# The fourth batch of a fused FFT filter and expert layer does two steps of its last stage per slot, and counts and places in one slot

## The chip, the cores and the metric

The kernel runs on one core of one Trainium2 chip. The metric is the device time of one execution in microseconds (us), the median of several runs. The profile is of one further execution. PE is TensorE, DVE is VectorE, ACT is ScalarE, POOL is GpSimd and SP is SyncE; SP does nothing here but start DMA transfers.

## The reference

Each of 8 batches holds 2496 tokens of 256 channels. A circular filter runs over the tokens of a batch, and every filtered token then goes to one of 8 experts.

```python
X = np.fft.rfft(x, axis=1)                       # x: 8 x 2496 x 256
y = np.fft.irfft(X * (filt_r + 1j*filt_i), n=2496, axis=1)
x = y.reshape(8*2496, 256)                       # 19968 tokens
logits = x @ w_gate + modality_bias[modality_id] # 8 experts
e_idx = np.argmax(logits, axis=1)
probs = softmax(logits); gate_w = probs[arange, e_idx]
for e in range(8):
    mask = e_idx == e
    h = np.maximum(x[mask] @ w1[e], 0.0)         # 256 -> 1024
    out[mask] = gate_w[mask, None] * (h @ w2[e]) # 1024 -> 256
```

## The kernel before, in words

The batches are numbered 0 to 7, so the fourth batch is batch 3. A batch of 2496 = 48 x 52 tokens passes through three stages of small transforms.

- **Stage 1** (13 steps): PE multiplies the input rows (L245), ACT moves the result out of PSUM (L249) and stores it to DRAM (`b1_d`, L252).
- **Stage 2** (12 pairs of frequencies, 13 steps): SP loads `t2` back from `b1_d` (L534), PE transforms forward (`forward`, L551), ACT evicts (L578), DVE multiplies by the filter (L585, L586), PE transforms back (`inverse`, L563 and L564), ACT evicts `z` (L614) and stores it to `b2_d` (L616).
- **Stage 3** (10 working steps and 2 that drain): SP loads `t4` from `b2_d` (L540, four pieces of 8, 8, 8 and 2 columns, each good for three steps, the last for one). Each step does four matmuls (L688, L691) into a PSUM tile, scales it into the token rows `yo` (DVE L726 in even steps, ACT L724 in odd ones), transposes the tokens of the step before (PE L711, DVE copy `yT` L720), and adds the gate's logits of the step before that (PE L716, DVE L729).

Then the routing of the batch: **count** (`counting`, L737 to L757, a chain of small DVE operations over all 20 columns of logits: maximum, one-hot, running count `c`), **place** (`placing`, L763 to L785: a pair of matmuls L765 and L766 that sums `c` over the partitions into the PSUM tile `psO`, then positions on DVE; the exponential on ACT, L767), and **table** (`tabling`, L832 to L868: which blocks of 256 tokens are full). After it, POOL scatters the batch's 20 tiles of tokens into the bins of the experts in DRAM (`bins_d`, L806, an indirect DMA each, of 128 rows of 520 bytes).

The **experts** take blocks of 256 tokens from the bins: SP loads `xs` (L914), PE transposes (L951), DVE copies (L952) and copies the block's first weight matrix (L933), PE multiplies (`up`, L965), ACT applies the ReLU (L970), PE multiplies again (`down`, L978), DVE scales by the gate weight into `osb` (L990), and POOL writes the rows out (L992, an indirect DMA).

Batches 0 to 2 pass through another form of the stages first. From there a loop over slots `n` interleaves what is left (at the end of the code below). In each slot one step of stage 1 of a batch, one of stage 2 of an earlier one, one of stage 3 of a still earlier one, some scatters and one or two of the experts' steps are issued. `begin[g]` is a batch's first slot, -15 for batch 3 and `(g-4)*14` for the later ones; stage 2 begins `OFF2` = 17 slots later and stage 3 `OFF3` = 34 slots later. So batch 3 has its stage 3 in slots 19 to 30, counts in slot 31, and places and tables in slot 32; its scatters are issued in slots 32 to 45. Batch 4 begins stage 3 in slot 34. The experts take two steps per slot before slot 24 and 1.25 on average from there on (`EARLY`, `STEPS`).

The slot loop gives the work in program order; a scheduler then sets the order on each engine from it, and waits on semaphores tie the engines together. DMA transfers started by ACT and SP take one of eight semaphore lanes in turn (DMAHW0 to DMAHW7); a new transfer on a lane waits until the one before it on that lane has landed. The scatters have lanes of their own (DMASW0 to DMASW7). The stages share one PSUM pool, `ps`, of three buffers: stage 1, both transforms of stage 2, the step of stage 3, its transposes with the logits, and `psO` all take their tile there, five tiles in a slot before (seven with two steps of stage 3). The tiles `t2` and `t4` share four SBUF buffers, and the routing's small tiles (`lg`, `c` and the others) have one buffer each.

Of the kernel before, what the change touches and what calls it, by code (L numbers as in the profile page):

```python
# [29 lines left out]
def kernel(  # L30
# [87 lines left out]
    TURNED = 2  # L118
# [99 lines left out]
    NPY = NY // EV  # L218
# [36 lines left out]
    def input_piece(g, k):  # L255

        stage1(g, k)
        if (k + 1) * EV in [t1 for t0, t1 in TCH]:
            load_x()
# [53 lines left out]
    def to_columns(g, q, on):  # L313

        t0 = q * TQ
        m = min(TQ, NTT - t0)
        if t0 % TCM == 0 and m < TQ and g == TURNED:
            st[g]["t4", t0 // TCM] = sp.tile([P, EV, DC, P], BF16, tag="yT", bufs=2, name="t4").rearrange(
                "p t a q -> p t (a q)")[:KA]
        elif t0 % TCM == 0:  # L320
            st[g]["t4", t0 // TCM] = bp.tile([KA, TCM, D], BF16, tag="t24", name="t4")
        pool, tag = (op, "tr") if g < TURNED else (pp, "ps")
        tt = pool.tile([P, EV * D], F32, tag=tag, name="tt").bitcast(BF16)
        tv = tt.rearrange("p (i a q) -> p i a q", i=TQ, a=DC)
        for i in range(m):
            for dc in range(DC):
                mm = nc.tensor.transpose(tv[:KA, i, dc, :], st[g]["zT"][:, dc, t0 + i, :], ident)
        marks["pe"].append(mm.ins)
        dst = st[g]["t4", t0 // TCM][:, t0 % TCM:t0 % TCM + m, :]
        evict(on, dst.rearrange("p t d -> p (t d)"), tt[:KA, 0:m * D])  # L330
# [198 lines left out]
    def load_t2(g, c, part=None):  # L529
        src = b1_d[g].rearrange("t (jr s) c -> (t jr) s c", jr=4)  # L530
        if part != 1:
            st[g]["t2", c] = bp.tile([KB, SCH, D], BF16, tag="t24", name="t2")
        a, b = {None: (0, KB), 0: (0, KA), 1: (KA, KB)}[part]
        nc.sync.dma_start(st[g]["t2", c][a:b], src[a:b, c * SCH:(c + 1) * SCH, :])  # L534

    def load_t4(g, c):
        t0, t1 = TCH[c]
        src = b2_d[g].rearrange("s (jr t) c -> (s jr) t c", jr=4)
        t4 = bp.tile([KA, TCM, D], BF16, tag="t24", name="t4")
        ins = nc.sync.dma_start(t4[:, 0:t1 - t0, :], src[:, t0:t1, :])  # L540
        st[g]["t4", c] = t4
        return ins
# [78 lines left out]
    def stage2(g, k):  # L621

        if k < NK:
            ps = forward(g, k)
        if k > 0:
            pz = inverse(g, k - 1)
        if k < NK:
            filtering(g, k, taken(g, k, ps))
        if k > 0:
            returned(g, k - 1, pz)  # L630
# [156 lines left out]
    def run(steps):  # L787

        for _ in steps:
            pass  # L790

    def count(g):

        run(counting(g))

    def place(g):

        run(placing(g))
# [307 lines left out]
    def routed(g):  # L1106

        place(g)
        to_bins.append([g, 0])

    def tabled(g):

        run(tabling(g, KR[g], g == B - 1))
# [8 lines left out]
    with tc.manual_schedule(engines={ET.PE, ET.Activation, ET.DVE}):  # L1122
# [141 lines left out]
        n = -2 * LONG  # L1264
# [31 lines left out]
    OFF3 = OFF2 + NS // EV + 1 + 4  # L1296
    begin = [(g - TURNED - 2) * GAP for g in range(B)]
# [3 lines left out]
    CHORES = [3, 3, 3, 3]  # L1301
    AFT = len(COLS)
    LEAD = 2
    end = begin[B - 1] + OFF3 + NPY + 3
    assert opening and opening[0][0] == 0
    n = max(0, opening[0][1] + WAIT)
# [3 lines left out]
    n = 0  # L1310
# [3 lines left out]
    while n <= end or to_bins or opening:  # L1314
        for g in range(TURNED + 2, B):
            if 0 <= n - begin[g] < NP:
                input_piece(g, n - begin[g])
        for g in range(TURNED + 1, B):
            k = n - begin[g] - OFF2
            if k + LEAD in (-2, -1):  # L1320
                load_t2(g, 0, k + LEAD + 2)
            if (k + LEAD) % 4 == 0 and 0 < k + LEAD < NS // EV:
                load_t2(g, (k + LEAD) // 4)
            if 0 <= k <= NS // EV:
                stage2(g, k)
        if n < AFT:
            for q in COLS[n]:
                to_columns(TURNED, q, "vs"[q % 2])
                moe.step()
        for k in (2 * (n - AFT), 2 * (n - AFT) + 1):  # L1330
            if 0 <= k < NPY:
                stage3(TURNED, k, "vs"[k % 2])
        some(CHORES[n] if n < len(CHORES) else 2)
        for g in range(TURNED + 1, B):
            k = n - begin[g] - OFF3
            if (k + LEAD) % 3 == 0 and 0 <= k + LEAD < NPY:
                load_t4(g, (k + LEAD) // 3)
            if 0 <= k <= NPY + 1:
                stage3(g, k)
            if k == NPY + 2:  # L1340
                count(g)
            if k == NPY + 3:
                routed(g)
                tabled(g)
        if n <= end:
            pace(pace(2) if n % 2 or n < GAP else 1)
            owed += EARLY if n < 24 else STEPS
        else:
            pace(1 if n % 4 else 0)
            owed += FT // FQ  # L1350
        while owed >= 1:
            owed -= 1
            moe.step()
        n += 1
# [44 lines left out]
```

## Time and profile before

| | |
|---|---|
| median of 3 runs | 556.67 us (556.52 to 557.93) |
| profiled execution | 559.18 us, of which the span of the profile is 557.3 us |
| busy share of the span | PE 89%, DVE 67%, ACT 68%, POOL 70% |
| mean granted clock of TensorE | 0.957 |
| DMA | 89.86 MB, mean 161 GB/s |

The span is the time from the first to the last instruction of the profile; 1.9 us of the profiled execution lie outside it. The clock is given as a share of full speed (2.4 GHz); 0.5 is the lower of its two levels. A row of the timeline is one instruction, or several alike that follow each other on one engine (x4), with the start in us from the span's beginning and the time that it or they took; in brackets stands how long the engine sat idle before it and what ended that. PE's matmuls are pipelined: what one costs is the distance to the next start (0.11 us for 256 columns at the full clock), not its own duration. Idle time of an engine that is not the bottleneck costs nothing.

### The profile page before, as it was taken

What the parts mean: (1) busy time and instruction counts of PE and PEld (TensorE: products, weight loads), DVE (VectorE), ACT (ScalarE), POOL (GpSimd) and SP (SyncE); (2) the same over time, 40 slices, a digit from 0 to 9 for tenths busy, and PEclk for the clock granted to TensorE, in tenths of its full rate; (3) what the DMA queues carried; (4) which work ended last, traced back from release to release, by engine and by line L of the source; (5) the groups of instructions that cost most, each with busy time, mean ns of one, the idle gap of its engine ahead of it and who ended that gap; (6) DMA issues with size and microseconds to landing.
All of it is one profiled execution on the core that took longest, in us unless ns stands there. A gap on an engine that the chain in (4) does not pass through costs nothing. (4 is left out here: it accounts for less than half of the span.)

```text
span 557.3 us, 14900 instructions
## 1 busy us (share of the span) xinstructions
PE 494.1 (89%) x5012; PEld 451.8 (81%) x5012; DVE 375.1 (67%) x1130; ACT 376.3 (68%) x694; POOL 391.5 (70%) x427
## 2 busy tenths in 40 slices
PE   3788797979999699999879999898998999979994
PEld 2677686769889588999768899897988899979993
DVE  8867968746765466797767897877554465565551
ACT  4686785845888668888678777454656666656662
POOL 9743588785578732468776777777777777777775
PEclk9979888879999889999989999998999999999998
DMA  9989979778677898988886764623544445347532
GB/s 140 164 147 205 199 143 167 174 155 172 170 172 186 198 237 183 213 234 222 213 251 196 189 187 131 185 88 110 149 110 111 124 114 125 92 129 154 133 105 71
DMA packets 98265, 89.86 MB, mean 161 GB/s; under 512 B 40151, under 2 KB 81591, under 8 KB 98095
## 3 DMA queue, kind: packets, MB, share of 16 engines
q0 software_dynamic: 30112, 50.75, 40.0%
q1 hardware_dynamic: 44773, 26.60, 19.7%
q10 hardware_dynamic: 23302, 11.50, 7.7%
q8 instruction: 44, 0.72, 0.5%
q14 instruction: 34, 0.28, 0.2%
HBM read 58.82 MB, written 45.07 MB: 186 GB/s over the span
## 5 line engine op out<-in xcount | busy, mean ns | idle before, releaser
L970 ACT ACTIVATE hT<-hps 128x512 f16<-128x512 f32 x316 | 186.9, 599 | 99.8 <-PE hps L965 95.9
L992 POOL DMA_INDIRECT out_dram<-osb,metas x158 | 165.6, 1048 | 68.5 <-DVE osb L990 30.5
L806 POOL DMA_INDIRECT bins_d<-yo,pos_i x160 | 167.8, 1049 | 57.7 <-issue 26.0
L965 PE MATMUL hps<-xT,w 128*128 128x256 f16 x1264 | 199.4, 277 | 7.3 <-ACT hT L970 2.6
L965 PEld LDWEIGHTS <-w 128*128 128x128 f16 x1264 | 149.3, 145 | 14.6 <-issue 7.0
L978 PEld LDWEIGHTS <-hT 128*128 128x128 f16 x1264 | 123.7, 99 | 17.2 <-issue 5.5
L978 PE MATMUL ops<-w2sb,hT 128*128 x704 | 113.1, 275 | 0.9 <-issue 0.7
L990 DVE TENSOR_SCALAR osb<-ops,metas 128x256 f32<-128x256 f32 x158 | 69.8, 477 | 51.9 <-DMA out_dram<-osb,metas 30.5
L978 PE MATMUL ops<-w,hT 128*128 128x256 f16 x560 | 83.3, 272 | 3.2 <-DVE osb L990 3.1
L933 DVE COPY w<-w1sb 128x2048 f16 x79 | 56.0, 709 | 32.9 <-PE hps L965 30.1
L578 ACT CAST xf<-ps 104x512 f16<-104x512 f32 x96 | 57.2, 596 | 10.2 <-PE ps L551 9.2
L585 DVE TENSOR_TENSOR p<-xf,g 104x512 f16<-104x512 f16 x96 | 40.4, 421 | 25.4 <-ACT xf L578 25.1
L614 ACT CAST z<-pz 104x512 f16<-104x512 f32 x60 | 35.4, 591 | 12.8 <-PE pz L564 8.4
L586 DVE TENSOR_TENSOR xf<-xf,g 104x512 f16<-104x512 f16 x96 | 40.5, 422 | 2.5
L551 PE MATMUL ps<-t,w2m 104*104 104x256 f16 x192 | 38.8, 285 | 1.8 <-ACT t L249 0.7
L249 ACT CAST t<-ps 96x512 f16<-96x512 f32 x52 | 30.3, 582 | 13.4 <-PE ps L245 8.8
L688 PE MATMUL ps<-t,wbm 96*128 96x256 f16 x120 | 29.4, 277 | 4.8 <-DMA t<-b_d 4.4
L952 DVE COPY xT<-pT 128x512 f16<-128x512 f16 x44 | 18.6, 422 | 22.3 <-PE pT L951 22.2
L563 PE MATMUL pz<-p,a1m 104*104 104x256 f16 x120 | 30.4, 273 | 1.9 <-DVE p L585 1.7
L164 POOL DMA_DIRECT2D xt<-in_x_dram x32 | 23.5, 735 | 11.4 <-PE ps L551 8.1
L564 PE MATMUL pz<-xf,a2m 104*104 104x256 f16 x120 | 29.4, 272 | 0.9 <-DVE xf L586 0.5
L691 PE MATMUL ps<-t,wbm 96*128 96x256 f16 x108 | 27.0, 277 | 0.0
(231 smaller groups left out, 777.2 us busy)
## 6 DMA issues: line engine op xcount, KB each, us to landing
xt<-in_x_dram POOLq DMA_DIRECT2D x24, 384.0 KB
t<-b_d SPq DMA_DIRECT2D x19, 384.0 KB
b_d<-z ACTq DMA_DIRECT2D x30, 208.0 KB
xs<-bins_d SPq DMA_DIRECT2D x44, 130.0 KB
b_d<-t ACTq DMA_DIRECT2D x24, 192.0 KB
t<-b_d SPq DMA_DIRECT2D x11, 416.0 KB
w1sb<-in_moe_w_dram POOLq DMA_DIRECT2D x16, 256.0 KB
w2sb<-in_moe_w_dram POOLq DMA_DIRECT2D x8, 512.0 KB
```

Source lines behind the costliest of these rows:

```text
L551: mm = nc.tensor.matmul(ps[:KB, i, :], lhsT=w2m[:, s + i, :], rhs=st[g]["t2", s // SCH][:, s % SCH + i, :], start=True, stop=True)
L578: nc.scalar.copy(xf, ps[:KB])
L585: nc.vector.tensor_mul(p1, xf, g1[:, sl, :])
L586: nc.vector.tensor_mul(xf, xf, g2[:, sl, :])
L614: nc.scalar.copy(st[g]["z"][:, k % 2], pz[:KB])
L806: ins = nc.gpsimd.indirect_dma_start(out=bins_d[:, :], out_offset=IOA(ap=st[g]["pos"][:rows, t:t + 1], axis=0), in_=st[g]["yw"][:rows, t, ...
L933: cp = nc.vector.tensor_copy(b["w1"].rearrange("p a f -> p (a f)"), w1sb[:, ds(ej, 1)].rearrange("p o a f -> p (o a f)"))
L965: mm = nc.tensor.matmul(hps[:, k, :], lhsT=b["w1"][:, dc, ft:F:FT], rhs=b["xT"][:, dc].rearrange("p i t -> p (i t)"), start=(dc == 0), sto ...
L970: nc.scalar.activation(b["hT"][:, q * FQ:(q + 1) * FQ, :], hps, AF.Relu)
L978: nc.tensor.matmul(b["ops"][:, i, :], lhsT=b["hT"][:, ft, i * P:(i + 1) * P], rhs=b["w2"][:, ft, :] if b["still"] else w2sb[:, ds(b["e"], ...
L990: nc.vector.tensor_scalar_mul(osb[:, i, :], b["ops"][:, i, :], gate[:, i, :])
L992: ins = nc.gpsimd.indirect_dma_start(out=out[:, :], out_offset=IOA(ap=b["meta"][:, i, 0:1], axis=0), in_=osb[:, i, :], in_offset=None, bou ...
```

## The change

Batch 3 alone (`g == TURNED + 1`) now takes the steps 2k and 2k+1 of its stage 3 in the slot in which it took step k, and the two steps behind stage 3 (count; place and table) in one slot too. Its stage 3 lies in slots 19 to 24, and count, place and table in slot 25; the scatters are issued in slots 25 to 37. The loads of its `t4` are issued two slots ahead as before, now in slots 17, 18, 20 and 21 in place of 17, 20, 23 and 26. The other batches keep one step per slot, and the experts' steps per slot are the same. Every engine has the same instructions in both kernels.

```diff
     LEAD = 2
+
+    def last_of(g, m):
+
+        k = m - begin[g] - OFF3
+        return (k,) if g > TURNED + 1 else (2 * k, 2 * k + 1)
+
     end = begin[B - 1] + OFF3 + NPY + 3
...
         for g in range(TURNED + 1, B):
-            k = n - begin[g] - OFF3
-            if (k + LEAD) % 3 == 0 and 0 <= k + LEAD < NPY:
-                load_t4(g, (k + LEAD) // 3)
-            if 0 <= k <= NPY + 1:
-                stage3(g, k)
-            if k == NPY + 2:
-                count(g)
-            if k == NPY + 3:
-                routed(g)
-                tabled(g)
+            for k in last_of(g, n + LEAD):
+                if k % 3 == 0 and 0 <= k < NPY:
+                    load_t4(g, k // 3)
+            for k in last_of(g, n):
+                if 0 <= k <= NPY + 1:
+                    stage3(g, k)
+                if k == NPY + 2:
+                    count(g)
+                if k == NPY + 3:
+                    routed(g)
+                    tabled(g)
```

What that does to the engines' order is seen at three places. In the rows, what stands left of an arrow is written and what stands right of it is read; a number behind a name is a buffer's.

**First place: batch 3's count on DVE**, from the maximum (L737) to the count `c` (L754). Before, in slots 31 and 32:

```order
L737 TENSOR_REDUCE mx<-lg 128x20
L933 ISA
L933 COPY w_4442<-w1sb 128x2048
L990 TENSOR_SCALAR osb<-ops,metas 128x256 x2
L739 TENSOR_TENSOR oh<-lg,mx 128x160
L741 TENSOR_TENSOR oh<-oh,revio 128x160
L757 TENSOR_TENSOR lg<-lg,mx 128x160
L743 TENSOR_REDUCE wm<-oh 128x20
L585 TENSOR_TENSOR p_4403<-xf,g_68 104x512
L746 TENSOR_TENSOR ohT<-oh,wm 128x20x8
L586 TENSOR_TENSOR xf<-xf,g_69 104x512
L748 MEMSET ohT 32x8x2
```

Behind these, before, come L952, L751, L954 and L754. The changed kernel, in slot 25:

```order
L737 TENSOR_REDUCE mx<-lg 128x20
L739 TENSOR_TENSOR oh<-lg,mx 128x160
L741 TENSOR_TENSOR oh<-oh,revio 128x160
L757 TENSOR_TENSOR lg<-lg,mx 128x160
L743 TENSOR_REDUCE wm<-oh 128x20
L746 TENSOR_TENSOR ohT<-oh,wm 128x20x8
L784 TENSOR_REDUCE ssum<-lg 128x20
L748 MEMSET ohT 32x8x2
L785 RECIPROCAL yo_107<-ssum 128x20
L751 SCALAR_TENSOR_TENSOR sc<-keep,ohT 128x160
L645 TENSOR_TENSOR lg<-mids,biasd 128x160
L754 COPY c<-sc 128x8
```

The work of stage 2 and of the experts between the steps of the count is gone; three small operations of routing (L784, L785, L645) stand among them in its place.

**The same place on PE**, up to the matmuls that read `c`. Before:

```order
L978 LDWEIGHTS hT
L978 ISA
L978 MATMUL ops<-w2sb,hT 128x256
L765 MATMUL psO<-c,Lexcl 128x8
L766 MATMUL psO<-c,ones_sq 128x8
```

Between the last logits of batch 3 (L716) and L765, 47 matmuls stand on PE before: 12 of stages 1 and 2, and 35 of the experts'. In the changed kernel:

```order
L978 MATMUL ops<-w2sb,hT 128x256
L951 LDWEIGHTS xs
L951 MATMUL pT<-ident,xs 128x128
L765 MATMUL psO<-c,Lexcl 128x8
L766 MATMUL psO<-c,ones_sq 128x8
```

There 13 matmuls are left between them: two L245, two L551, four L563 and L564, four L978 and one L951.

**Second place: the first step of batch 5's stage 3 on PE** (slot 48; `t4_5274` is its first piece), with the semaphores that it waits for. On ACT, ahead of two ReLU evictions that PE needs, stands in both kernels the store `L616 DMA b2_d<-z_5257`, which waits for lane DMAHW6. Before:

```order
L965 LDWEIGHTS w1_5194
L965 MATMUL hps_5493<-xT_5197,w1_5194 128x256
L688 LDWEIGHTS wbm_64 [waits DMAHW6_49]
L688 MATMUL ps_5439<-t4_5274,wbm_64 128x256 [waits Activation_49]
L691 LDWEIGHTS wbm_64
L691 MATMUL ps_5439<-t4_5274,wbm_64 128x256
```

In the changed kernel:

```order
L965 LDWEIGHTS w1_5195
L965 MATMUL hps_5493<-xT_5198,w1_5195 128x256
L688 LDWEIGHTS wbm_64 [waits DMAHW0_49]
L688 MATMUL ps_5439<-t4_5274,wbm_64 128x256 [waits Activation_49]
L691 LDWEIGHTS wbm_64
L691 MATMUL ps_5439<-t4_5274,wbm_64 128x256
```

The load of this piece has moved from lane DMAHW6 to lane DMAHW0; the store on ACT has stayed on DMAHW6, behind another transfer now.

**Third place: SP's queue**, where `t2_5004` (`t2_5011` in the changed kernel) is the first piece of batch 6's stage 2, loaded in two parts of 96 and 8 rows, and `xs_5414` is the first block of experts that batch 3's scatters fill. Before:

```order
L534 DMA t2_5004<-b1_d 8x2048 [waits DMAHW2_49,DMAHW0_49]
L540 DMA t4_5274<-b2_d 96x2048 [waits DMAHW5_49,DMAHW4_49,DMAHW6_49,DMAHW3_49,PE_49]
L534 DMA t2_5300<-b1_d 104x2048 [waits PE_49]
L893 TENSOR_LOAD bj_i_4514 [waits DVE_49]
L914 ISA
L914 DMA xs_5414<-bins_d 128x260 [waits DMASW5_49,DMASW4_49,DMASW6_49,DMASW3_49,DMASW7_49,DMASW2_49,DMAHW1_49,DMASW1_49,DVE_49]
```

In the changed kernel:

```order
L893 TENSOR_LOAD bj_i_4218 [waits DVE_49]
L914 ISA
L914 DMA xs_5414<-bins_d 128x260 [waits DMASW4_49,DMASW3_49,DMASW5_49,DMASW2_49,DMASW6_49,DMASW1_49,DMASW7_49,DMASW0_49,DMAHW2_49,DVE_49,PE_49]
L534 DMA t2_5011<-b1_d 8x2048 [waits DMAHW0_49]
L914 ISA
L914 DMA xs_5635<-bins_d 128x260 [waits DMAHW7_49,DVE_49,PE_49]
L540 DMA t4_5274<-b2_d 96x2048 [waits DMAHW6_49,DMAHW4_49]
```

The small part of batch 6's `t2` now stands behind the block load, and so behind the landing of batch 3's scatters.

## Rows read from the trace of the kernel before

**Rows 1.** Page, part 1: busy time (share of the span) xinstructions.

```profile
PE 494.1 (89%) x5012; PEld 451.8 (81%) x5012; DVE 375.1 (67%) x1130; ACT 376.3 (68%) x694; POOL 391.5 (70%) x427
```

**Rows 2.** Windows: length, busy PE, PEld, DVE, ACT, POOL, clock, DMA share, GB/s.

```profile
198.92:231.01 32.09, 31.98 (x338) 29.46 (x337) 21.91 (x64) 26.52 (x51) 11.13 (x11) 1.00 0.89 208
231.01:241.34 10.33, 9.98 (x93) 9.10 (x92) 9.44 (x44) 8.45 (x18) 5.11 (x6) 1.00 0.89 226
241.34:277.80 36.46, 35.74 (x374) 32.88 (x372) 28.65 (x95) 28.81 (x56) 28.53 (x31) 1.00 0.84 214
277.80:283.84 6.04, 3.49 (x18) 2.68 (x18) 4.10 (x22) 3.12 (x7) 4.76 (x6) 0.72 0.86 243
374.07:557.30 183.23, 165.55 (x1503) 153.82 (x1500) 101.11 (x224) 108.20 (x182) 139.19 (x133) 0.98 0.44 118
```

**Rows 3.** Timeline of PE, one step of batch 3's stage 3 in slot 26.

```profile
219.94 0.27 PE L688 MATMUL ps<-t,wbm 96*128 96x256 f16 x1
220.05 0.27 PE L691 MATMUL ps<-t,wbm 96*128 96x256 f16 x1
...
220.75 0.64 PE L965 MATMUL hps<-xT,w 128*128 128x256 f16 x4
```

**Rows 4.** Timeline of PE, batch 3's last logits and its psO.

```profile
229.78 0.24 PE L716 MATMUL lt<-wg,yT 128*128 128x8 f16 x4
...
235.44 0.36 PE L765 MATMUL psO<-c,Lexcl 128*128 128x8 f32 x2
```

**Rows 5.** Timeline of DVE, batch 3's count, first and last step.

```profile
230.06 0.17 DVE L729 TENSOR_TENSOR lg<-lg,lt 128x16 f32<-128x16 f32 x1 [0.73 <-PE lt L716]
...
235.04 0.24 DVE L754 COPY c<-sc 128x8 f32<-128x8 f32 x1
```

**Rows 6.** Timeline of PE, batch 7's last logits and its psO.

```profile
374.07 0.24 PE L716 MATMUL lt<-wg,yT 128*128 128x8 f16 x4
...
378.90 0.39 PE L765 MATMUL psO<-c,Lexcl 128*128 128x8 f32 x2 [2.37 <-DVE c L754]
```

**Rows 7.** Timeline of DVE, batch 7's count and the experts' work in it.

```profile
374.35 0.17 DVE L729 TENSOR_TENSOR lg<-lg,lt 128x16 f32<-128x16 f32 x1 [1.23 <-PE lt L716]
374.48 0.88 DVE L990 TENSOR_SCALAR osb<-ops,metas 128x256 f32<-128x256 f32 x2
375.27 0.31 DVE L737 TENSOR_REDUCE mx<-lg 128x20 f32<-128x160 f32 x1
375.50 0.68 DVE L933 COPY w<-w1sb 128x2048 f16 x1
376.10 0.32 DVE L739 TENSOR_TENSOR oh<-lg,mx 128x160 f32<-128x160 f32 x1
...
378.67 0.17 DVE L754 COPY c<-sc 128x8 f32<-128x8 f32 x1
```

**Rows 8.** Timeline of PE, ahead of batch 5's stage 3.

```profile
280.35 1.01 PE L965 MATMUL hps<-xT,w 128*128 128x256 f16 x4 [2.58 <-ACT hT L970]
...
282.23 0.42 PE L688 MATMUL ps<-t,wbm 96*128 96x256 f16 x1
```

**Rows 9.** Timeline of ACT, the same place (ACTq: ACT's DMA issue).

```profile
279.35 0.31 ACTq L616 DMA_DIRECT2D b_d<-z  x1
279.71 1.08 ACT L970 ACTIVATE hT<-hps 128x512 f16<-128x512 f32 x2 [2.62 <-DMA t<-b_d]
```

**Rows 10.** Timeline of SP, the last t2 part of batch 6 and the first block load.

```profile
261.55 0.31 SPq L534 DMA_DIRECT2D t<-b_d  x1
...
282.41 0.36 SPq L914 DMA_DIRECT2D xs<-bins_d  x1
```

**Rows 11.** Timeline of PE, the first step of batch 6's stage 2 (slot 45).

```profile
269.28 0.40 PE L551 MATMUL ps<-t,w2m 104*104 104x256 f16 x2
```

**Rows 12.** Timeline of POOL, batch 3's first and last scatter.

```profile
239.01 1.07 POOL L806 DMA_INDIRECT bins_d<-yo,pos_i  x1 [3.76 <-issue]
...
277.44 0.93 POOL L806 DMA_INDIRECT bins_d<-yo,pos_i  x1 [0.30 <-PE ps L551]
```

## The prediction

> **What bounds the kernel now.** I read the page's busy shares first, then windows cut at the places that the change touches, then the timelines of PE, DVE, ACT, SP and POOL there. PE leads with 89% of the span [rows 1], and the reader should look at what that hides: from 198.92 to 231.01, the eleven slots 20 to 30 in which batch 3 has its stage 3, PE is busy for 31.98 of 32.09 us, and after it for 9.98 of 10.33 and 35.74 of 36.46 [rows 2]. PE is full there, so work that moves inside these stretches gains nothing on PE; only waits of PE that come or go count. From 198.92 to 283.84 PE has one gap of size: 2.58 us in front of an `up` at 280.35, with ACT named [rows 8]. ACT sat idle 2.62 us itself, and that ended with a DMA on `t` [rows 9]: its store of `z` waits on its semaphore lane for the load of batch 5's first `t4` piece, and the two ReLU evictions queue behind the store. In the last window PE is busy 165.55 of 183.23 us at a clock of 0.98 [rows 2]; nothing there waits for batch 3, so a delay before it is passed on to the end, us for us.
>
> The profiled execution took 559.18 us, 1.9 of them outside the span, and the median of the runs is 556.67, 2.5 less. I make the sum against 559.18 and subtract 2.5 at the end.
>
> **The change part by part.**
>
> *Two steps per slot, slots 19 to 24.* A step of stage 3 costs PE 0.81 us (219.94 to 220.75) [rows 3], the mean slot there 32.09/11 = 2.92 us, so a doubled slot costs PE 3.73 us. ACT has 26.52 us in 51 instructions in the same window, 2.41 a slot and 0.52 an instruction [rows 2]; a second step adds half an instruction on the mean: 2.67. DVE has 21.91/11 = 1.99, and a second step, of which a slot had one already, adds under 1. PE stays the longest, and six steps that come early are six that need not be done later, so the work itself costs nothing. What is not free is the order: seven tiles now take turns in three `ps` buffers in a slot, and the two steps depend on each other (scale, transpose, copy, logits). I take +0.4, from 0 (the experts' matmuls between the steps cover it all) to 2 (one eviction of 0.52 us uncovered in four of the six slots).
>
> The trace has 0.11 us of PE idle in the whole window at five tiles a slot [rows 2], so the rotation holds there. The Trainium skill, page "Perfetto Trace Analysis", section "Matmuls", says that independent groups of matmuls should rotate through different PSUM banks so that the eviction of one overlaps the matmuls of the next. By it, more tiles per slot in the same three buffers speak against this part, and the upper end above would be the value; the trace can't show seven tiles, and I stay near the row that it has.
>
> *The lighter slots, 25 to 30.* Without its step a slot costs PE 2.92 - 0.81 = 2.11 us and ACT 2.41 - 0.26 = 2.15 [rows 2, 3]. The two are level, so that ACT decides now and then: 6 x 0.04 = 0.24, and I take +0.3, from 0 to 1.5 (a quarter us a slot, half an eviction).
>
> *Count and place in one slot.* This is the largest new cost. Before, 5.66 us of PE's matmuls lay between batch 3's last logits (229.78) and `psO` (235.44), and PE didn't wait, although DVE's chain to `c` took 230.06 to 235.04 [rows 4, 5]. Now 13 matmuls stand there, 13 x 0.11 [rows 3] = 1.43 us, and with the four small logits matmuls 1.53. The chain itself is shown by batch 7, whose count has the same order on DVE, L784 and L785 in it: L729 at 374.35, `c` at 378.67, 4.32 us. In it stand two pieces of experts' work that the new order has not, L990 with its successor at 375.27 (0.79 us) and L933 with its successor at 376.10 (0.60 us) [rows 7]. That leaves 2.93 us. In front come 0.28 us from the last logits to L729 and behind 0.23 from `c` to `psO` [rows 6, 7]; the new order adds L645, as wide as L739, which takes 0.32. Chain: 0.28 + 2.93 + 0.32 + 0.23 = 3.76 us. Less the cover of 1.53, PE waits 2.23 us if DVE is punctual, and longer if it comes late out of slot 24, where its own work has bunched. I take +2.6, from 2.0 to 3.9 for a DVE 1.7 us late (nearly its 1.99 us of a slot). Batch 7 shows the same wait at 2.37 us in front of its `psO` [rows 6]. Behind the waiting `psO` stand the rest of a block's transposes, stage 1 and an `up`, none of which needs it.
>
> *The clock behind such a wait.* After the 2.58 us gap nine matmuls from 280.35 to 282.23 take 0.21 us each in place of 0.11 [rows 8], and the window 277.80 to 283.84 has a clock of 0.72, where the 18 matmuls took 3.49 us [rows 2]; at 0.11 each they would take 1.98. So a wait of this length costs 1.5 us more. For the new one I take +1.5, from 0 (a wait broken in two) to 1.8.
>
> *The lane on ACT.* The load of batch 5's first `t4` piece now has another semaphore lane than the store on ACT, and the store's lane was last held by a store long landed. The 2.58 us in front of the `up` go: -2.6, from -2.9 to 0, and the 1.5 us of low clock behind it: -1.5, from -1.6 to 0. What is late next is the same load itself: PE reaches its first matmul, L688 at 282.23 before, nine matmuls after the gap's place, at 280.35 - 2.58 + 9 x 0.11 = 278.8 [rows 8], and the load landed by 279.35, when the store behind it could go [rows 9]. That is a wait of 0.6 us if the load keeps its place against PE; I take +0.5, from 0 to 2.6.
>
> *The queue of SP.* The small part of batch 6's first `t2`, issued at 261.55 before [rows 10] and needed at 269.28 [rows 11], now stands behind the block load that waits for batch 3's last scatter. The scatters run from 239.01 to 277.44 at POOL's own pace [rows 12] and start 3.57 us after `psO` [rows 4, 12]. In the new order `psO` comes some 9.6 us earlier, the last scatter so at about 268, the block load at about 270, the small part lands some 2 to 3 us later. Stage 2 of batch 6 starts at 269.28 plus what has been lost by then (0.4 + 2.6 + 1.5 + 0.3), about 274. So I take +0.2, with 2.7 as the upper end, if POOL falls behind or nothing is lost before. That the block load itself comes 12 us sooner is worth nothing: its block is not due for several slots.
>
> Sum: 0.4 + 0.3 + 2.6 + 1.5 - 2.6 - 1.5 + 0.5 + 0.2 = +1.4 us; 559.18 + 1.4 = 560.6 profiled, 558.1 as a median.
>
> **The rivals.**
>
> *The lane's wait stays or returns* (slower). The lanes are dealt out in order, and the load of `t4` is late in itself: if PE or ACT waits 2.6 us for it all the same, with the low clock behind, 2.6 + 1.5 - 0.5 come back: +5.0, or 561.7. For it speaks that the load landed only at 279.35 [rows 9], against it that it is on another lane by the order. It decides from a landing 2 us later against PE than now.
>
> *The new `psO` wait is hidden* (faster). If ACT or the matmuls before it delay PE anyway, or DVE runs ahead, only the lane's gain is left: 1.4 - 2.6 - 1.5 = -2.7, and -4 where the half slots cost nothing either: about 553.5. Against it stands batch 7, where PE had 2.46 us of work in front of `psO` (374.07 to 378.90, less the wait) and still waited 2.37 [rows 6].
>
> *Both waits are as before*: neither the new one nor the gain; 1.4 - 2.6 - 1.5 + 2.6 + 1.5 - 0.5 = +0.9, or 557.6. That is the case in which the change moves work inside a full PE and does nothing else.
>
> *The DMA engines are the bound.* They are busy 0.89 of the time in both stretches before 241.34, and 0.84 after [rows 2]. The scatters start 9.6 us earlier, eight of them (8 x 128 x 520 bytes = 0.53 MB, 2.4 us at 226 GB/s) fall into the stretch that is fullest. A load of stages 2 or 3 that lands 2.4 us late leaves PE waiting that long and at the low clock: 2.4 + 1.5 more, +5.3, or 562. That PE idles for only 0.11 us in that window [rows 2] speaks for slack in the loads. The Trainium skill, page "DMA: Bandwidth & Descriptors", section "Issuing engines are not separate DMA queues", says that transfers started by different engines run on the same 16 DMA engines and interleave; by it the scatters on POOL's queue do slow SP's loads, and the share of 0.89 is in keeping with it.
>
> **How the numbers follow.** My forecast, both the new wait and the lane's gain, has 0.50, with 558.1 and its own range of 556 to 560. The returned wait has 0.14, the hidden `psO` 0.20, no wait of either kind 0.08, the DMA engines 0.08. A difference of 0.3% (1.7 us) is about what a measurement can tell from no change: under 555.0 is faster, over 558.3 slower. Of the forecast's 0.50, 0.26 lies within the bound, 0.22 above it and 0.02 below. The hidden `psO` gives 0.19 to faster and 0.01 to same, the case with neither 0.07 to same and 0.01 to slower, the returned wait 0.14 to slower, and the DMA engines 0.06 to slower and 0.02 to same; together 0.21, 0.36 and 0.43. Since a bias of my added terms would point upwards (each was bounded at 0 below), I move 0.03 from slower to faster: 0.24, 0.36, 0.40. The range of 553.5 to 563 leaves out the ends of the faster and of the DMA case, about 2 in 10 together with an unnamed mishap.
>
> **What would show it.** In the profile of the changed kernel: a gap of PE in front of batch 3's L765 of 2 to 4 us, ended by `c` (L754), with matmuls at 0.21 us behind it; no gap over 0.5 us between slots 20 and 25; no gap over 1 us at ACT's store ahead of batch 5's stage 3, and a short one by DMA at its first L688; the first scatter some 9 us earlier; batch 6's first L551 without a wait. If L765 comes without a gap, or if the gap of 2.58 us is still there, the sum is wrong by the terms named.

## The result, and the profile after

| | before | changed |
|---|---|---|
| median of the runs | 557.08 us (556.52 to 557.93, 4 runs) | 565.92 us (561.90 to 568.59, 4 runs) |
| ratio to before | 1 | 1.0139, 95% interval 1.0098 to 1.0180 |
| profiled execution / span | 559.18 / 557.3 us | 565.49 / 563.6 us |

The change makes the kernel slower, by 1.4% as the ratio of the runs and by 8.8 us between the medians; forecast were +1.4 us and 558.1, in a range of 553.5 to 563. A second series gave 563.41 us (561.88 to 569.08) against 557.38 (555.14 to 561.37), ratio 1.0114 (1.0040 to 1.0188).

The windows below are cut at the starts of batches' forward matmuls, at the beginning of slots 18, 20, 31, 36, 45 and 53, first in the changed kernel, then in a second profile of it (from the second series). The columns are those of [rows 2].

```profile
184.31:200.20 15.89, 9.98 (x66) 7.92 (x65) 5.29 (x13) 6.15 (x12) 8.07 (x8) 0.69 0.81 226
200.20:239.44 39.24, 36.66 (x346) 32.70 (x345) 28.04 (x101) 26.81 (x51) 16.51 (x18) 0.91 0.70 155
239.44:252.63 13.19, 12.18 (x114) 10.97 (x113) 7.89 (x21) 10.23 (x21) 10.45 (x11) 1.00 0.94 262
252.63:279.42 26.79, 23.46 (x259) 21.92 (x257) 16.57 (x49) 21.23 (x42) 18.71 (x20) 0.99 0.91 219
279.42:303.56 24.14, 23.31 (x215) 21.11 (x216) 19.51 (x75) 18.61 (x37) 13.73 (x13) 0.94 0.79 219
```

```profile
186.18:200.08 13.90, 8.91 (x66) 7.22 (x65) 4.86 (x12) 6.00 (x12) 8.17 (x8) 0.75 0.83 234
200.08:238.04 37.96, 35.28 (x347) 31.52 (x346) 28.29 (x102) 26.95 (x52) 16.15 (x17) 0.96 0.74 168
238.04:251.83 13.79, 12.00 (x115) 10.95 (x114) 8.20 (x21) 10.33 (x21) 10.74 (x12) 1.00 0.94 243
251.83:276.99 25.16, 23.47 (x259) 21.91 (x257) 16.56 (x49) 21.23 (x42) 18.50 (x20) 1.00 0.92 226
276.99:300.48 23.49, 22.48 (x214) 20.10 (x215) 19.41 (x75) 18.45 (x37) 13.72 (x13) 1.00 0.81 237
```

The lengths answer to these of the kernel before, cut in the same way:

```profile
186.04:198.92 12.88, 8.23 (x59) 6.47 (x58) 4.55 (x11) 5.52 (x11) 8.24 (x8) 0.73 0.85 223
...
231.01:245.40 14.39, 13.95 (x129) 12.67 (x128) 13.50 (x58) 11.40 (x24) 8.26 (x9) 1.00 0.87 239
245.40:269.28 23.88, 23.49 (x259) 21.91 (x258) 17.10 (x53) 20.36 (x41) 18.70 (x21) 1.00 0.88 211
269.28:297.23 27.95, 23.55 (x216) 20.91 (x215) 19.82 (x76) 19.14 (x38) 20.68 (x22) 0.94 0.79 228
```

with 32.09 us in the second place [rows 2]. The reader should compare lengths, not PE's busy shares: slots 20 to 30 hold nearly the same matmuls (338 before, 346 and 347 after) and grow from 32.09 to 39.24 and 37.96 us, although PE is called busy for 93% of them. They are not quite the same matmuls: eight of stage 3 (four 256 columns wide, four 128) lie in slot 19 now, and twelve of the experts' have come over from slots 31 to 35 together with the four of `psO`. From slot 53 on the kernels run alike: before, the last forward matmul comes 41.96 us after slot 53's, changed 41.74.

PE in slot 25 of the changed kernel, where [rows 4] had no wait:

```profile
222.78 0.22 PE L951 MATMUL pT<-ident,xs 128*128 128x128 f16 x1
225.23 0.57 PE L765 MATMUL psO<-c,Lexcl 128*128 128x8 f32 x2 [2.23 <-DVE c L754]
...
226.78 1.06 PE L965 MATMUL hps<-xT,w 128*128 128x256 f16 x4
```

The wait is where it was forecast and 2.23 us long; `c` is copied at 224.92, 3.2 us after the last L729 at 221.69. Behind it the four matmuls of L965 take 0.85 us in place of 0.44, and this lasts until about 231: two matmuls of L965 at 230.62 still have 0.21 us each, twelve of L978 from 231.04 have 0.12. In the second profile the wait is 2.23 us too, and the matmuls at 0.21 us last from 226.4 to 229.7.

The first step of stage 3, in slot 19, and the first forward matmul of batch 6, in slot 45:

```profile
194.25 0.40 PE L688 MATMUL ps<-t,wbm 96*128 96x256 f16 x1 [3.96 <-DMA t<-b_d]
...
279.42 0.64 PE L551 MATMUL ps<-t,w2m 104*104 104x256 f16 x2 [2.73 <-issue]
```

and SP's queue ahead of the latter, to be read beside [rows 10] and [rows 11]:

```profile
268.06 0.30 SPq L534 DMA_DIRECT2D t<-b_d  x1
268.47 0.36 SPq L540 DMA_DIRECT2D t<-b_d  x1
272.38 0.36 SPq L914 DMA_DIRECT2D xs<-bins_d  x1
272.80 0.40 SPq L534 DMA_DIRECT2D t<-b_d  x1
```

The small part of `t2` goes out right behind the block load, at 272.80, and PE reaches its matmul near 276.7; the matmul starts 6.6 us after the issue. In the second profile the same queue issues the part at 271.46, the matmul starts 5.5 us later, at 276.99, and PE waits 0.5 us there: this wait changes from one execution to the next.

On ACT, the store that waited in [rows 9] no longer does:

```profile
287.78 0.31 ACTq L616 DMA_DIRECT2D b_d<-z  x1
288.14 1.08 ACT L970 ACTIVATE hT<-hps 128x512 f16<-128x512 f32 x2 [0.15 <-ACT lg L767]
```

The load of batch 5's first `t4` piece has moved too. Before, SP issued it here:

```profile
274.51 0.30 SPq L540 DMA_DIRECT2D t<-b_d  x1
```

and in the changed kernel 9.3 us later:

```profile
283.85 0.30 SPq L540 DMA_DIRECT2D t<-b_d  x1
```

### The profile page after: what moved, and what is told of

The parts are those of the page before. It is cut to its first block, busy times and chain, and to the rows that moved or that the text cites. A ratio compares the mean times of both kernels' runs of the same rounds, so it can differ in the third digit from the quotient of the medians.

```text
span 563.6 us, 14892 instructions
## 1 busy us (share of the span) xinstructions
PE 499.5 (89%) x5012; PEld 456.0 (81%) x5012; DVE 375.5 (67%) x1130; ACT 376.2 (67%) x694; POOL 392.2 (70%) x427
## 5 line engine op out<-in xcount | busy, mean ns | idle before, releaser
L992 POOL DMA_INDIRECT out_dram<-osb,metas x158 | 167.5, 1060 | 75.1 <-DVE osb L990 28.9
L965 PE MATMUL hps<-xT,w 128*128 128x256 f16 x1264 | 200.7, 279 | 5.5 <-DVE xT L952 2.6
L965 PEld LDWEIGHTS <-w 128*128 128x128 f16 x1264 | 150.2, 146 | 12.0 <-issue 3.3
L978 PEld LDWEIGHTS <-hT 128*128 128x128 f16 x1264 | 124.1, 99 | 16.0 <-issue 4.0
L978 PE MATMUL ops<-w2sb,hT 128*128 x704 | 114.7, 278 | 0.7 <-issue 0.6
L978 PE MATMUL ops<-w,hT 128*128 128x256 f16 x560 | 83.4, 273 | 2.3 <-DVE osb L990 2.2
L585 DVE TENSOR_TENSOR p<-xf,g 104x512 f16<-104x512 f16 x96 | 40.3, 420 | 18.9 <-ACT xf L578 18.4
L551 PE MATMUL ps<-t,w2m 104*104 104x256 f16 x192 | 40.1, 293 | 4.5 <-issue 2.7
L688 PE MATMUL ps<-t,wbm 96*128 96x256 f16 x120 | 29.5, 277 | 5.1 <-DMA t<-b_d 4.5
L563 PE MATMUL pz<-p,a1m 104*104 104x256 f16 x120 | 30.9, 275 | 2.3 <-DVE p L585 2.1
L952 DVE COPY xT<-pT 128x512 f16<-128x512 f16 x44 | 18.6, 422 | 20.9 <-PE pT L951 20.8
L564 PE MATMUL pz<-xf,a2m 104*104 104x256 f16 x120 | 29.7, 274 | 1.4 <-DVE xf L586 1.1
L720 DVE COPY yT<-lt 128x512 f16<-128x512 f16 x50 | 21.0, 421 | 10.3 <-PE lt L716 8.1
```

The source lines that it names most:

```text
L551: mm = nc.tensor.matmul(ps[:KB, i, :], lhsT=w2m[:, s + i, :], rhs=st[g]["t2", s // SCH][:, s % SCH + i, :], start=True, stop=True)
L585: nc.vector.tensor_mul(p1, xf, g1[:, sl, :])
L965: mm = nc.tensor.matmul(hps[:, k, :], lhsT=b["w1"][:, dc, ft:F:FT], rhs=b["xT"][:, dc].rearrange("p i t -> p (i t)"), start=(dc == 0), sto ...
L978: nc.tensor.matmul(b["ops"][:, i, :], lhsT=b["hT"][:, ft, i * P:(i + 1) * P], rhs=b["w2"][:, ft, :] if b["still"] else w2sb[:, ds(b["e"], ...
L992: ins = nc.gpsimd.indirect_dma_start(out=out[:, :], out_offset=IOA(ap=b["meta"][:, i, 0:1], axis=0), in_=osb[:, i, :], in_offset=None, bou ...
```

## The experiments

Theory A: the loss is a sum of single waits (`psO`, batch 6's `t2`, the longer wait in slot 19), less the lane's gain. Theory B: the doubled slots and the light ones behind them cost the time, and the waits are where it shows. The first series and one more (the usual chip below) ran at 557 us; in the other four the kernel before itself took 674 to 685 us, so from those only ratios are used. All ratios are to the kernel before of the same series, with 95% intervals:

| kernel | usual chip | chip at 674 to 685 us |
|---|---|---|
| changed | 1.0139 (1.0098 to 1.0180), 1.0114 (1.0040 to 1.0188) | 1.0073 (1.0023 to 1.0124) |
| steps doubled, count and place late | 1.0106 (1.0050 to 1.0161) | 1.0044 (0.9997 to 1.0092) |
| loads early only | | 0.9998 (0.9956 to 1.0040) |
| changed, place in slot 27 | | 1.0102 (1.0054 to 1.0151) |
| changed, small part of `t2` first | | 1.0149 (1.0081 to 1.0217) |
| changed, both repairs | 1.0084 (1.0058 to 1.0111) | 1.0059 (1.0026 to 1.0092) |
| before, lane only | 1.0001 (0.9975 to 1.0027) | |
| both repairs, experts' steps moved | | 1.0075, 1.0040, 1.0147 |
| before, count and place in slot 31 | | 0.9989, 0.9981 |

**Steps doubled, count and place late.** Stage 3 doubled, the routing in its old slots.

```diff
-        return (k,) if g > TURNED + 1 else (2 * k, 2 * k + 1)
+        if g > TURNED + 1 or k > NPY + 1:
+            return (k,)
+        return tuple(j for j in (2 * k, 2 * k + 1) if j <= NPY + 1)
```

> Stage 3 of batch 3 doubled in slots 19 to 24 as in the changed kernel, but count back in slot 31 and place and table in slot 32. Theory A (the loss is a sum of single waits: psO in slot 25 with the low clock behind it 5.2 us, batch 6's t2 behind the block load 4.0, the longer wait in slot 19 2.2, less the lane's gain of 4.1): no gap at psO, no gap of 2.7 us ahead of batch 6's first L551, but the load of batch 5's t4 is again on lane DMAHW6, so ACT's store waits again; 559 to 561, about 1.004 to 1.008 of before. Theory B (the doubled slots and the bunched loads cost the time, wherever it shows): 563 or more, as the changed kernel.

> Doubled steps alone, count in slot 31 and place in slot 32, on this call's chip. Theory A (a sum of single waits): about 5 us under the changed kernel, 559 to 561 on a chip at 557, with ACT's wait of 2.6 us behind the lane of batch 5's t4 as in the kernel before. Theory B (doubled slots): within 1.5 us of the changed kernel.

On the usual chip 563.4 us, the same as the changed kernel of that series (563.41), although there is no wait at `psO` and none at batch 6's first matmul: theory B's number, not the 559 to 561 of theory A. Its windows, slots 20 to 30 and 31 to 35, then the last (slots 45 to 52):

```profile
197.32:232.40 35.08, 32.43 (x330) 28.55 (x328) 25.51 (x77) 25.73 (x50) 12.14 (x13) 1.00 0.80 186
232.40:251.34 18.94, 16.46 (x128) 14.40 (x129) 10.82 (x46) 11.22 (x22) 7.61 (x9) 0.82 0.79 201
...
274.60:298.54 23.94, 22.67 (x217) 20.10 (x215) 19.73 (x76) 18.79 (x38) 18.70 (x20) 1.00 0.87 240
```

The doubled and light slots take 35.08 us with eight matmuls fewer than before, without any low clock: 3.0 us lost, some 3.7 with the missing matmuls (4 x 0.11 and 4 x 0.055, the narrower ones). The last 1.0 of them is already the next thing: PE reaches batch 5 before its load, and a wait that the kernel before hasn't got comes in, with the low clock behind it (4.6 us more in slots 31 to 35). Without these 5.6 us the run would have come to about 557.8, so that it equals the changed kernel is in part chance, and by itself it doesn't decide between the theories. It shows that the doubled and light slots cost some 2.6 us with no wait at `psO`, and that another wait can come in where one is taken out. Its waits of PE in slots 25 to 30, and its timeline at slot 31:

```profile
PE ps L245 <- ACT t L249: 0.9, 1, 0.9
PE pz L564 <- DVE xf L586: 0.3, 1, 0.3
```

```profile
232.40 0.42 PE L551 MATMUL ps<-t,w2m 104*104 104x256 f16 x2 [1.02 <-DMA t<-b_d]
234.42 1.44 PE L978 MATMUL ops<-w2sb,hT 128*128 x6 [1.60 <-issue]
```

**Loads early only.** The kernel before, with the `t4` loads of batch 3 in the changed kernel's slots.

```diff
-            if (k + LEAD) % 3 == 0 and 0 <= k + LEAD < NPY:
-                load_t4(g, (k + LEAD) // 3)
+            for j in (2 * (k + LEAD), 2 * (k + LEAD) + 1) if g == TURNED + 1 else (k + LEAD,):
+                if j % 3 == 0 and 0 <= j < NPY:
+                    load_t4(g, j // 3)
```

> The kernel before with one step of stage 3 per slot, only the t4 loads of batch 3 issued in slots 17, 18, 20 and 21. Theory A: the second load behind the first lengthens the wait for t4 in slot 19 by 0.7 us and the low clock behind it by as much again, nothing else changes: 557.5 to 559. Theory B, if the early loads are what bunches: 561 or more.

0.9998: the early loads by themselves cost nothing within 0.4%, on the slower chip. There slots 18 and 19 take 6.1 us in this run and 6.1 to 6.4 in the kernel before, against 12.9 on the usual chip, and PE doesn't wait for the `t4` load at all, so the longer wait in slot 19 was not tested by it.

**Each repair alone.** Place and table in slot 27; or the small part of batch 6's `t2` ahead of the block load.

```diff
-                if k == NPY + 3:
+                if k == NPY + 3 + (4 if g == TURNED + 1 else 0):
```

```diff
-        nc.sync.dma_start(st[g]["t2", c][a:b], ...)
+        marks["t2", part] = [nc.sync.dma_start(st[g]["t2", c][a:b], ...).ins]
...
-            lds = [nc.sync.dma_start(b["xs"], ...)]
+            with tc.issue_after(marks["t2", 1][0]) if (tab[2], j) == (TURNED + 1, 0) else nullcontext():
+                lds = [nc.sync.dma_start(b["xs"], ...)]
```

> The changed kernel with count in slot 25 as there, but place and table in slot 27: 49 matmuls between the last logits and psO in place of 13. Theory A: the gap of 2.2 us in front of psO and the low clock behind it go, all else stays: about 5 us less than the changed kernel, 560 to 561. Theory B: the wait reappears at another place in slots 25 to 30, no gain over 1.5 us.

> The changed kernel with one order turned: the small part of batch 6's first t2 is issued on SP ahead of the block load that waits for batch 3's scatters. Theory A: the gap of 2.7 us ahead of batch 6's first L551 and the low clock behind it go, about 3 to 4 us less than the changed kernel, 561.5 to 563. Rival: the larger part of that t2, itself issued late (it waits for batch 6's stage 1), is what PE waits for: no change.

Both removed the wait that they aimed at (in the first, `psO` follows the matmul before it by 0.11 us, in the second the 2.23 us at `psO` stay and batch 6's first matmul comes without a wait), and neither brought the time back. On that chip the sizes can't be told, and the changed kernel itself didn't run in that series.

**Both repairs.**

> The changed kernel with both repairs: place and table in slot 27, and the small part of batch 6's t2 ahead of the block load on SP. Theory A: neither the gap at psO nor the one ahead of batch 6's L551, and the lane's gain kept: 555 to 558 on a chip at 557, about 8 us under the changed kernel. Theory B: over 562.

> Place in slot 27 and the small part of t2 first, on the chip of this call. The first run gave 1.0084. If these two waits are worth the 1 to 2 us that the median showed and not the 8 that their gaps show in the profile: 1.007 to 1.010. If they are worth their gaps: under 1.003.

On the usual chip 562.24 us, ratio 1.0084: just inside theory B's "over 562", far from A's 555 to 558. Both waits are gone and about a quarter of the loss with them (0.0030 of 0.0114, with intervals that overlap). The windows, slots 18 to 52:

```profile
186.48:200.18 13.70, 9.01 (x67) 7.31 (x66) 4.88 (x12) 6.02 (x12) 8.07 (x8) 0.75 0.86 240
200.18:236.18 36.00, 34.06 (x345) 30.03 (x343) 28.05 (x102) 26.30 (x51) 13.94 (x15) 1.00 0.77 177
236.18:249.58 13.40, 12.19 (x116) 11.22 (x115) 7.88 (x21) 10.45 (x22) 10.48 (x11) 1.00 0.88 233
249.58:273.58 24.00, 23.30 (x260) 21.91 (x258) 16.54 (x49) 20.78 (x42) 18.99 (x20) 1.00 0.90 228
273.58:299.40 25.82, 22.41 (x216) 19.86 (x215) 19.58 (x75) 19.06 (x38) 16.24 (x16) 1.00 0.87 238
```

Slots 20 to 30 still take 3.9 us more than 32.09, at the full clock and without the wait at `psO`; some 0.8 of them go to ten matmuls of the experts and four of `psO` that it has more there, less eight of stage 3. In its light slots PE now stands behind ACT and DVE:

```profile
223.84 0.38 PE L245 MATMUL ps<-xt,w1m 96*96 96x256 f16 x2 [0.89 <-ACT t L249]
224.32 0.38 PE L551 MATMUL ps<-t,w2m 104*104 104x256 f16 x2
...
225.25 0.31 PE L563 MATMUL pz<-p,a1m 104*104 104x256 f16 x1
225.82 0.27 PE L564 MATMUL pz<-xf,a2m 104*104 104x256 f16 x1 [0.26 <-DVE xf L586]
```

**Lane only.** The kernel before, with one 64-byte DMA behind the load of batch 5's first `t4`.

```diff
-                load_t4(g, (k + LEAD) // 3)
+                ins = load_t4(g, (k + LEAD) // 3)
+                if (g, k + LEAD) == (TURNED + 3, 0):
+                    with tc.issue_after(ins.ins):
+                        nc.sync.dma_start(mb_sb, moe_modality_bias...)
```

> The kernel before with one tiny DMA (64 bytes, a row that is loaded again and not read) on SP right behind the load of batch 5's first t4, so that ACT's store no longer shares that load's lane. If the lane is worth what I took: the 2.6 us of ACT and PE at 277.8 and the low clock go, a wait of under 1 us for the load comes in their place: 552.5 to 554.5 on a chip at 557. If the store is late for another reason: 556.5 to 557.5.

557.81 against 557.38 us: no gain. The wait ahead of batch 5's stage 3 is gone (the store goes out at 274.77, 2.4 us behind the load, and PE takes the two `up` and the first step one after the other), but slots 45 to 52 take 27.50 us, hardly less than before (27.95). The lanes behind the added DMA have moved on by one, and the next store of ACT shares its lane with a block load:

```profile
283.90 0.31 ACTq L616 DMA_DIRECT2D b_d<-z  x1
284.26 0.60 ACT L970 ACTIVATE hT<-hps 128x512 f16<-128x512 f32 x1 [2.54 <-DMA xs<-bins_d]
```

**Experts' steps moved to the light slots** (with both repairs).

```diff
-            owed += EARLY if n < 24 else STEPS
+            owed += STEPS if 19 <= n < 25 else 15 / 8 if 25 <= n < 31 else EARLY if n < 24 else STEPS
```

> Both repairs of the run before (place in slot 27, the small part of t2 first), and the experts' steps moved from the doubled slots to the light ones: 1.25 per slot in slots 19 to 24 in place of 2, 1.875 in slots 25 to 30 in place of 1.25; the sum is the same. Theory L (the light slots lose 2 to 3 us because PE has too little beside the three evictions of stages 1 and 2 that share three PSUM buffers): the loss in slots 25 to 30 falls from 3 to 1 us or less, and the time to 558 to 560. Rival P (ACT is the limit there: every experts' step brings an eviction of its own): no gain, 562 or more.

> The experts' steps moved from the doubled slots to the light ones, with place in slot 27 and the small part of t2 first, again, since the chip of the call before took 674 us for the kernel before (ratio there 1.0075). On a chip at 557: theory L (PE lacks work beside the evictions in the light slots): 557 to 560, loss of PE in slots 25 to 30 down from 3 to about 1 us. Rival P (ACT's evictions are the limit): 562 or more, no less than the 562.2 of the run with both repairs.

> The same with the experts' steps moved from the doubled slots to the light ones. Theory L (PE lacks work beside the evictions in the light slots): 0.3 to 0.6% less than the run with both repairs of this call. Rival P (ACT's evictions are the limit): the same within 0.2%, or slower.

1.0075, 1.0040 and 1.0147, all on the slower chip, the last beside 1.0059 for both repairs alone: inconclusive. The edit also did less than its name says. PE has 66 matmuls of the experts (L965, L978) in slots 25 to 30, against 62 with both repairs alone, and 71 against 76 in slots 20 to 24, so the light slots got hardly any more work; in them PE waits 1.5 us for DVE's product (L585) in place of the 0.9 for ACT. Theory L (PE lacks work) is not shown, nor is its rival that ACT is the limit.

**Count, place and table in slot 31**, one step of stage 3 per slot.

```diff
-            if k == NPY + 3:
+            if k == NPY + 3 - (g == TURNED + 1):
```

> The kernel before with count, place and table of batch 3 all in slot 31, one step of stage 3 per slot. 45 matmuls lie between the last logits and psO in place of 13 in the changed kernel. If the wait at psO comes from the short cover alone: no gap over 0.5 us there, and the load of batch 5's first t4 is off the store's lane: 553 to 557. If count and place in one slot cost time of themselves (DVE has 50 operations more in the slot): 558 to 560.

> The kernel before with count, place and table of batch 3 all in slot 31, again (ratio 0.9989 on the slow chip). Cover theory (45 matmuls ahead of psO hide the chain): 555.5 to 557.5, no gap over 0.5 us at psO. Against it (DVE's crowd in one slot costs by itself): 558 to 560.

0.9989 and 0.9981, intervals from 0.9941 to 1.0037: with 45 matmuls in front of `psO` (the distance to the matmul before it is 0.30 us), one slot for the routing costs nothing that can be measured.

**The kernel before and the changed one again.**

> The changed kernel itself once more, as the measure for the others of this call, since the chip of the call before took 684 us for the kernel before in place of 557. On a chip at 557 us: 562 to 568, ratio 1.010 to 1.018, with gaps of PE of about 2.2 us at batch 3's psO and about 2.7 us ahead of batch 6's first L551. On a slow chip: ratio 1.01 to 1.015.

> The changed kernel as the control of this call: ratio 1.010 to 1.015 on a chip of either speed.

> The kernel before, profiled a second time. The first profile has 2.58 us of wait ahead of batch 5's stage 3 with 1.5 us of low clock, and its execution took 559.2 us where the median is 557.1. If that wait is there in every execution, the lane's gain of 4 us in the changed kernel is real and other costs must be larger than I summed: the wait again between 2 and 3 us. If it is an accident of that execution: under 1 us here and an execution near 557.

> The kernel before, profiled a third time (the second was on a chip at 677 us). The first profile has 2.58 us of wait ahead of batch 5's stage 3 and an execution 2 us over the median. If the wait is the usual case: 2 to 3 us again. If it belongs to the slower executions alone: under 1 us, and an execution of 556 to 557.5.

> The kernel before, profiled once more. On a chip at 557: if the wait of 2.58 us ahead of batch 5's stage 3 is the usual case, 2 to 3 us again; if it belongs to the slower executions, under 1 us. On a slow chip its place can't be told, since every engine waits more there.

The changed kernel came as expected in the second series in its time and in the wait at `psO`, not in the wait ahead of batch 6's first matmul (0.5 us in place of 2.7); on the slower chip it gave 1.0073, under the expected 1.010 to 1.015. The three profiles of the kernel before all fell on the slower chip (678, 677 and 674 us), so whether its wait at 277.8 is there in every execution at 557 us stays open.

## Why the prediction was wrong

Right were the direction of the sum and the wait that it put first. Point by point, on the usual chip (the two profiles of the changed kernel, stretch by stretch against the one before):

| slots | forecast | first profile | second profile |
|---|---|---|---|
| 18 and 19 | 0 | +3.0 | +1.0 |
| 20 to 30 | +4.8 (0.4, 0.3, 2.6, 1.5) | +7.2 | +5.9 |
| 31 to 35 | 0 | -1.2 | -0.6 |
| 36 to 44, with batch 6's first matmul | +0.2 | +2.9 | +1.3 |
| 45 to 52 | -3.6 (-2.6, -1.5, 0.5) | -3.8 | -4.5 |
| sum | +1.4 | +8.1 | +3.1 |

The stretches don't hold quite the same matmuls. With each matmul put in at its distance to the next start at the full clock (0.109 us for 256 columns, 0.055 for 128, 0.027 for 8, 0.07 and 0.11 for L765 and L766; an estimate from the timelines), the same work took +2.4, +6.1, +0.4, +3.0 and -3.8 us in the first profile, +0.4, +4.9, +1.0, +1.3 and -4.5 in the second.

*The step that failed is the cost of the doubled and the light slots*, taken at 0.4 and 0.3 us, and above all that of the light ones. By the terms of the sum without `psO`, its low clock and batch 6's `t2`, the kernel with both repairs should have taken 2.9 us less than the kernel before (0.4 + 0.3 - 2.6 - 1.5 + 0.5); it took 4.9 more. Where the wait at `psO` is absent, slots 20 to 30 cost 3.9 us more with both repairs (36.00 against 32.09) and 3.0 in the steps-only kernel; for the same work, estimated as above and without the 1.0 us that the latter waits for batch 5's load at the end, 3.1 and 2.6. The light slots have most of it: 2.3 and 1.8 us against 0.3, over the upper end of 1.5, while the doubled ones have 0.8 to 0.9, inside their range. The windows show it in PE's idle time too (length less busy time): 0.04 us in the light slots before, 1.64 with both repairs, 2.33 in the steps-only kernel with that 1.0. Slots 20 to 24 and 25 to 30 of the kernel before:

```profile
198.92:216.12 17.20, 17.12 (x179) 15.83 (x178) 12.12 (x34) 14.33 (x28) 6.54 (x7) 1.00 0.87 221
216.12:231.01 14.89, 14.85 (x162) 13.63 (x161) 9.79 (x30) 12.18 (x23) 4.58 (x5) 1.00 0.92 192
```

of the kernel with both repairs:

```profile
200.18:221.24 21.06, 20.77 (x233) 18.55 (x231) 14.95 (x45) 15.81 (x30) 6.62 (x7) 1.00 0.64 161
221.24:236.18 14.94, 13.30 (x114) 11.48 (x113) 13.10 (x58) 10.49 (x22) 7.33 (x9) 1.00 0.95 199
```

and slots 25 to 30 alone of the steps-only kernel, then of the changed one in its second profile:

```profile
218.42:232.40 13.98, 11.65 (x99) 9.99 (x98) 10.43 (x33) 9.92 (x21) 5.30 (x7) 1.00 0.95 198
```

```profile
221.16:238.04 16.88, 14.54 (x116) 12.96 (x116) 13.34 (x58) 11.14 (x23) 9.54 (x11) 0.90 0.87 179
```

In the changed kernel itself this loss doesn't come on top of the wait at `psO`; the wait stands in its place. Slots 25 to 30 cost it 5.1 and 4.0 us for the same work, and the 2.23 us with the low clock behind them (2.9 and some 1.7) make up all of that. When place moves to slot 27, the wait goes and the light slots' own waits appear: 16.88 us become 14.94, where the sum's terms would have taken off the whole 4.1. The sum added two costs that hide each other.

I had compared sums of busy time per slot, 2.11 us of PE against 2.15 of ACT, and called them level. What the rows suggest to decide is the order within a slot: in slots 25 to 30 all three tiles of stages 1 and 2 in the `ps` pool (stage 1, forward, inverse) are emptied by ACT, and PE's next tile waits for one of them (0.89 us at 223.84), or for DVE's product (0.26 at 225.82). Before, the tiles of stage 3, most of them emptied by DVE, stood between, and PE had their matmuls to do. That the light slots lose about 2 us is measured; that this order is why is read from these rows, which name 1.2 us of it, and no run that gave PE the filler back has tested it. The Trainium skill, page "Perfetto Trace Analysis", section "Optimization Strategy", says that a gap that repeats on the engine that should be full can mean too few buffers for the next tile. The wait of L245 for ACT is one for a tile, but it is a single one of 0.89 us, and it comes in the slots with fewer tiles, not in the doubled ones, where I had looked for it.

*The wait at `psO`* was right: 2.6 forecast, 2.23 in both profiles, as the chain less its cover gave without lateness of DVE. That it is the same to the hundredth is luck: the chain took 4.2 us (221.03 to 225.23) in place of 3.76, and the matmuls in front 2.0 in place of 1.53. *The low clock behind it* was mis-sized in the first profile: 5.8 us at the lower level (225.23 to 231.0) cost 2.9 us in place of 1.5; in the second it was shorter, 3.4 us at a cost of some 1.7 (clock 0.96 over slots 20 to 30 in place of 0.91).

*The lane* was right in size and only in part in cause. Slots 45 to 52 are 3.8 and 4.5 us shorter, but the steps-only kernel, whose load and store share the lane as before, is shorter there by 4.0, and the kernel before with the lane freed by only 0.5. In the first the store comes 5.4 us behind the load, when that has landed (it landed 4.8 us after its issue before), in place of the 2.4 at which ACT was ready for it before:

```profile
276.84 0.30 SPq L540 DMA_DIRECT2D t<-b_d  x1
```

```profile
282.21 0.31 ACTq L616 DMA_DIRECT2D b_d<-z  x1
282.57 1.09 ACT L970 ACTIVATE hT<-hps 128x512 f16<-128x512 f32 x2 [0.15 <-ACT lg L767]
```

In the second another store waits for another load. In the changed kernel both count: the load goes out 9.3 us later itself, the store 3.9 and 3.6 us behind it, so with a landing after 4.8 us a shared lane would still have cost it about 1 us (an estimate). Most of the 4 us is therefore not a gain of the lane but time that was waited there before and that a kernel gets back whose stores come later behind their loads. That is the second reason why the repairs bring so little: with both, the delay at slot 45, counted from slot 18, is 3.9 us in place of 7.6, and only 2.1 of them are given back (25.82 against 27.95), where the changed kernel got 4.5.

*The queue of SP* was mis-sized and varies: 0.2 forecast, 2.7 us of wait in one profile, 0.5 in the other. The last scatter came as forecast (267.58 against about 268), but the block load went out at 272.38 in place of about 270, and batch 6's first matmul came 6.6 and 5.5 us after the issue of the small part, whose landing I had put at 2 to 3. *Slot 19* stood in no term: the `t4` load is waited for in every profile on the usual chip, 3.10 us before and 3.96 and 3.50 after, with two `t4` loads issued back to back, and in the first profile the matmuls behind it run at 0.21 us for 6.0 us in place of 3.4; whether the early loads are the cause stays open.

The rivals: that the new wait would be hidden, and that neither wait would change, are out. The returned wait didn't come: in neither profile of the changed kernel do PE or ACT wait for the `t4` load ahead of batch 5's stage 3. The DMA engines as a bound: in slots 20 to 30 their share fell from 0.89 to 0.70, so it is not that which stretched them.

What stays open: the second profile explains 3.1 us, the median of that series has 6.0. The kernel before was profiled in an execution 2.1 us over its median, so some of its stretches are too long. The profile of the lane-only kernel (556.24 us) says where: slots 20 to 35 are alike there (32.15 and 14.37 us), slots 18 and 19, 36 to 44 and 45 to 52 are shorter by 0.5, 0.7 and 0.5 and what lies ahead of slot 18 by 1.0. So the losses in slots 20 to 35 don't hang on that execution; the rest is not settled.

## What to carry to other kernels

Steps that look like load may be the filler between evictions (read from the rows here, not proved): before thinning a slot, ask which engine empties the tiles that are left in it, and whether they all wait for the same one. Waits don't add up: one can stand where another would have been, as at `psO`, and a stretch that waits for a transfer can give back part of what was lost before it and take back what was won, so a repair is worth its gap only if nothing else waits in its place, there or downstream. Freeing one transfer from a shared semaphore lane moves the sharing to the next pair; look at who has it then.

## What was not expected of the hardware

In four of the five series that I ran, the kernel before took 674 to 685 us in place of 557. Its profile there has PE busy for 79% of a span of 672.4 us, not 89%, and the waits of ACT for "remote" releasers, absent at 557 us, are 38.2 us; DMA moved 134 GB/s in place of 161. What makes that chip slower is not shown.

```profile
PE 532.5 (79%) x5012; PEld 469.1 (70%) x5012; DVE 378.6 (56%) x1130; ACT 373.4 (56%) x694; POOL 379.0 (56%) x427
```

```profile
ACT hT L970 <- remote: 38.2, 14, 5.1
```
